# Spreading k's inverse norms through a DRAM row, and a new order of loads and PSUM buffers in the front

## Chip, cores and metric

One core of one Trainium2 chip runs the whole kernel. The metric is the device time of one execution in microseconds (us); the median of several runs counts.

## The reference

Two parts follow each other. A cross-covariance attention works on `q`, `k`, `v` of shape 4 x 6016 x 256 (batch, rows, channels), and a gated feed-forward layer works on its output, seen as 24064 x 256.

```python
def _attn_ref(q, k, v, tau):
    qn = q / (np.linalg.norm(q, axis=1, keepdims=True) + 1e-06)
    kn = k / (np.linalg.norm(k, axis=1, keepdims=True) + 1e-06)
    s = kn.transpose(0, 2, 1) @ qn / tau
    s = s - s.max(-1, keepdims=True)
    a = np.exp(s)
    a /= a.sum(-1, keepdims=True) + 1e-09
    return (v @ a).astype(np.float32)

def _moe_ref(x, w_gate, w_val, w_out):      # w_gate, w_val 256 x 1536, w_out 1536 x 256
    gate = 1.0 / (1.0 + np.exp(-(x @ w_gate)))
    val = x @ w_val
    return (gate * val @ w_out).astype(np.float32)
```

The norms run over the rows, so that there is one per channel and batch: 256 for q and 256 for k. The score matrix `s` is only 256 x 256 per batch. `tau` is 1.

## The kernel before

**Per batch.** The kernel computes the scores `q^T k` of a batch in PSUM (`ps_s`), squares q and k and sums the squares over the rows (`acc`, then a matmul with ones, `ps_n`). The root of the four columns of sums is `r` (128 partitions x 4: two columns for q, two for k), and `norms_inv` (L350) turns it into 1/(norm + 1e-6). q's inverse norm is a factor per partition of `ps_s`. k's inverse norm is a factor per column, so it has to be spread: every partition needs the whole row of 256 values. `scale_x` (L287) multiplies by both, `exps` (L388) takes the exponential, `row_sums` (L397) sums the rows, and twelve products `gh` (L452) multiply the exponentials with the two weight matrices. Thus G = a·w_gate and H = a·w_val are small matrices per batch, and v meets them directly.

**Per chunk.** v of a batch comes in 12 chunks (`ci`) of 4 x 128 rows, the last of 3 x 128. `load_v` (L144) loads a chunk on GpSimd's DMA queue, `transpose_v` (L458) transposes it, in all chunks but the first two by a transposing DMA on SP. For each of 12 blocks of 128 features (`f`), `glu` (L480) issues two gate matmuls into `ps_gate`, two value matmuls into `ps_val`, a tanh on ScalarE (`g_sb`, L501) and a multiply on VectorE (`hT`, L502). `ps_gate` and `ps_val` have two buffers each. The output product of the chunk before is spread over the same blocks, seven 128-column matmuls in each (`run_work`). It uses a scheme with fewer products, which needs sums of parts of `hT` on VectorE (`a_sum`, L524; in every block but f = 0 and f = 2) and additions on GpSimd.

**Order.** The instructions of each engine run in the order in which the program issues them. That order is written out by hand: `side_work` (L731) gives each piece of the next batch's attention a slot, and slot 12·ci + f is issued after block f of chunk ci. Scores, squares and sums of the next batch are done in chunks 0 to 7. From slot s0 = 98 on, so in chunk 8, follow the norms, in chunk 9 the spread and the exponentials, and up to the last block of chunk 11 the products `gh`, which must be there when the next batch begins. In this text (9,6) is block 6 of chunk 9. Batches 1, 2 and 3 are prepared in this way.

**The spread before.** `spread_both` (L300) multiplies r's column, broadcast over 128 columns, with a float32 identity, twice, on TensorE; `copy_rk` (L312) copies the result from PSUM into `rk_sb` on ScalarE. Batch 0 has functions of its own, `spread_k` and `weights`, and is prepared in the front, before any feed-forward work exists.

**The front.** All of q and k of batch 0 has to be loaded first (L151 to L177), then the first v chunk (L178), then the weights (L182 to L187), all on GpSimd's queue in this order. The first v chunk is transposed on TensorE into `ps_tp`, half of it is copied out by VectorE and half by ScalarE (L471 to L475, L723). `ps_tp` comes from the pool `psv` of two PSUM buffers, from which two of the first `gh` products (L727, L728) also take theirs. `row_sums` of the first half is issued between the transposes and VectorE's copy (the argument `then`, L474).

**PSUM.** Eight banks: two each for `psg`, `psv` and `pso`, and one each for `pss` (the scores, later half of the `gh` products) and `psm` (norms, the spread, row sums, the other half).

Of the kernel before, what the change touches and what calls it, by code (L numbers as in the profile page):

```python
# [9 lines left out]
FP32 = mybir.dt.float32  # L10
BF16 = mybir.dt.bfloat16
# [42 lines left out]
def kernel(  # L54
# [20 lines left out]
    nc = tc.nc  # L75
    P = nc.NUM_PARTITIONS
# [4 lines left out]
    B, N, C = q.shape  # L81
# [3 lines left out]
    CB = C // P  # L85
# [3 lines left out]
    TPC = 4  # L89
# [7 lines left out]
    def rows(x, b):  # L97
        return x[b].rearrange("(p t) c -> p t c", p=P)
# [3 lines left out]
    def pool(name, bufs, **kw):  # L102
        return ctx.enter_context(tc.tile_pool(name=name, bufs=bufs, **kw))
# [11 lines left out]
    spool = pool("spool", 1)  # L115
    mpool = pool("mpool", 2)
    opool = pool("opool", 2)
    psg = pool("psg", 2, space=PSUM)
    psv = pool("psv", 2, space=PSUM)
    pso = pool("pso", 2, space=PSUM)  # L120
    pss = pool("pss", 1, space=PSUM)
    psm = pool("psm", 1, space=PSUM)
# [3 lines left out]
    def mm(out, lhsT, rhs, start, stop, **kw):  # L126
        nc.tensor.matmul(out, lhsT=lhsT, rhs=rhs, start=start, stop=stop, **kw)  # L127
# [4 lines left out]
    def load_qk(b, t0, nt):  # L132

        tiles = []
        for name, src in (("q", q), ("k", k)):
            tl = qkpool.tile([P, 2 * TPC, C], BF16, tag=name, name=name + "_sb")
            nc.gpsimd.dma_start(out=tl[:, :nt, :], in_=rows(src, b)[:, t0 : t0 + nt, :])
            tiles.append(tl)
        for u in range(0, nt, TPC):
            qk[b, t0 + u] = [tl[:, u : u + TPC, :] for tl in tiles]  # L140
# [3 lines left out]
    def load_v(b, ci):  # L144
        t0, nt = groups[ci]
        v_sb = vpool.tile([P, TPC, C], BF16, tag="v", name="v_sb")
        nc.gpsimd.dma_start(out=v_sb[:, :nt, :], in_=rows(v, b)[:, t0 : t0 + nt, :])
        vs[b, ci] = v_sb
# [16 lines left out]
    ident_f = consts.tile([P, P], FP32)  # L165
# [9 lines left out]
    nc.scalar.copy(qk[0, 0][1], first_f32[1])  # L175
    for t0, nt in loads0[1:]:
        load_qk(0, t0, nt)  # L177
    load_v(0, 0)  # L178

    w_sb = [[consts.tile([P, CB, FG], BF16, name=f"w_{n}{fg}") for fg in range(NFG)] for n in ("gate", "val")]  # L180
    w_out_sb = consts.tile([P, FC, C], BF16)
    for fg in range(NFG):  # L182
        for w, src in enumerate((moe_w_gate, moe_w_val)):
            nc.gpsimd.dma_start(
                out=w_sb[w][fg],
                in_=src.rearrange("(t p) f -> p t f", p=P)[:, :, ds(fg * FG, FG)],
            )  # L187
    load_v(0, 1)

    w_sums = consts.tile([P, len(B_SUMS), FC // 2, P], BF16)  # L190
# [2 lines left out]
    for n in range(FC // TPC):  # L193
        w_f32[n] = f32pool.tile([P, TPC, C], FP32, tag="f32", name="w_f32")
        nc.gpsimd.dma_start(
            out=w_f32[n], in_=moe_w_out.rearrange("(t p) c -> p t c", p=P)[:, n * TPC : (n + 1) * TPC, :]
# [16 lines left out]
    st = {}  # L213

    def invert(out, x, eps, num):
        nc.vector.tensor_scalar(out=out, in0=x, scalar1=eps, scalar2=None, op0=ALU.add)
        nc.vector.reciprocal(out, out)
# [80 lines left out]
        )  # L298

    def spread_both(b):  # L300
        s = st[b]
        s["rk_ps"] = psm.tile([P, C], FP32, tag="m", name="ps_rk")
        for i in range(CB):
            mm(
                s["rk_ps"][:, ds(i * P, P)],
                s["r"][:, CB + i : CB + i + 1].to_broadcast([P, P]),
                ident_f,
                True,
                True,
            )  # L310

    def copy_rk(b):  # L312
        s = st[b]
        s["rk_sb"] = attp.tile([P, C], FP32, tag="rk", name="rk_sb")
        nc.scalar.copy(s["rk_sb"], s["rk_ps"])

    def norms_sqrt(b):
        s = st[b]
# [78 lines left out]
    def row_sums(b, i0, ni, pl, tag):  # L397
        s = st[b]
        ps_r = pl.tile([P, ni], FP32, tag=tag, name="ps_r")
        for i in range(ni):  # L400
            for j in range(CB):
                mm(
                    ps_r[:, i : i + 1],
                    s["e"][i0 + i][:, j, :],
                    ones_bf[:, 0:1],
                    start=(i == 0 and j == 0),
                    stop=(j == CB - 1),
                    skip_group_check=True,
                )
        r = attp.tile([P, ni], FP32, tag=f"rrow{i0}", name="rrow", bufs=2)  # L410
        invert(r, ps_r, 1e-9, 1.0)
        s.setdefault("rrow", []).extend(r[:, i : i + 1] for i in range(ni))
# [6 lines left out]
    def gh_tiles(b):  # L419
        st[b]["gh"] = [  # L420
            [ghpool.tile([P, CB, FG], BF16, tag=f"{n}{fg}", name=f"gh_{n}{fg}") for fg in range(NFG)]
            for n in ("G", "H")
        ]
# [28 lines left out]
    def gh(b, n, pl, tag, act=None):  # L452
        gh_store(b, n, gh_mms(b, n, pl, tag), n % 2 == 0 if act is None else act)
# [1 line left out]

    vts = {}

    def transpose_v(b, ci, ps=None, late=None, then=None):  # L458

        t0, nt = groups[ci]  # L460
        v_sb = vs.pop((b, ci))
        vT = vtpool.tile([P, TPC * CB, P], BF16, tag="vT", name="vT")
        flat = v_sb[:, :nt, :].rearrange("p t c -> p (t c)")
        if ps is None:
            nc.sync.dma_start_transpose(out=vT[:, : nt * CB, :], in_=flat)
        else:
            for n in range(nt * CB):
                nc.tensor.transpose(
                    out=ps[:, n, :], in_=flat[:, ds(n * P, P)], identity=ident_bf
                )  # L470
            half = nt * CB // 2 if late else nt * CB  # L471
            if late:
                late(vT[:, half : nt * CB, :], ps[:, half : nt * CB, :])
                then()  # L474
            nc.vector.tensor_copy(out=vT[:, :half, :], in_=ps[:, :half, :])  # L475
        vts[b, ci] = vT.rearrange("p (u cb) n -> p cb u n", cb=CB)

# [203 lines left out]
    for g, (t0, nt) in enumerate(groups0):  # L681
# [6 lines left out]
        while adds:  # L688
            w, last_sq = adds.pop()
# [26 lines left out]
    weights(0, 0)  # L716
    weights(0, 1)
    late = []
    ps_tp = psv.tile([P, TPC * CB, P], BF16, tag="v", name="ps_tp")
    gh_tiles(0)  # L720
    transpose_v(0, 0, ps_tp, lambda *a: late.append(a), lambda: row_sums(0, 0, 1, psm, "m"))
    gh(0, 0, psg, "g", act=True)
    nc.scalar.copy(*late.pop())  # L723
    half_row(0)
# [6 lines left out]
    def side_work(b):  # L731


        side = {}

        def at(slot, fn, *a):
            side.setdefault(divmod(slot, FC), []).append((fn, a))

        for ci in range(NCH):
            nb, nci = (b, ci + 1) if ci + 1 < NCH else (b + 1, 0)  # L740
            lb, lci = (b, ci + 2) if ci + 2 < NCH else (b + 1, ci + 2 - NCH)
            if (nb, nci) == (0, 1):
                at(8, lambda: transpose_v(0, 1, psm.tile([P, TPC * CB, P], BF16, tag="m", name="ps_tp")))
            elif nb < B:
                at(ci * FC + 2, transpose_v, nb, nci)
            if lb < B:
                at(ci * FC + 0, load_v, lb, lci)
            if (b, ci) == (0, 0):
                for i in range(FC // TPC):
                    at(8, copy_w_out, i)  # L750
                for n, m in enumerate((1, 0, 3, 2, 4)):
                    for i in range(FC // TPC):
                        at(10 + 2 * n, sum_w_out, m, i)
        n = b + 1
        if n == B:
            return side
        first, last = (14 if b == 0 else 0), 8 * FC
        for g, (t0, nt) in enumerate(groups):
            s0 = first + g * (last - first) // NCH
            if b == 0:  # L760
                at(max(0, s0 - 12), load_qk, n, t0, nt)
            elif s0 >= 24:
                at(s0 - 24, load_qk, n, t0, nt)
            for u in range(nt):
                at(first + (t0 + u) * (last - first) // NT, score, n, t0, u)
            if g == 0:
                at(s0, acc_start, n)
            for i, (fn, w) in enumerate(((acc_square, 0), (acc_add, 0), (acc_square, 1), (acc_add, 1))):
                at(s0 + 1 + 2 * i, fn, n, g, w)
        if n + 1 < B:  # L770
            for g, (t0, nt) in enumerate(groups[:3]):
                at(NCH * FC - 24 + 8 * g, load_qk, n + 1, t0, nt)
        s0 = 8 * FC + 2
        at(s0, norms_mm, n)
        at(s0 + 1, root_seed, n)
        at(s0 + 1, root_steps, n)
        at(s0 + 9, norms_inv, n)
        at(s0 + 10, spread_both, n)
        at(s0 + 11, copy_rk, n)
        at(s0 + 12, scale_x, n, 0)  # L780
        at(s0 + 13, scale_x, n, 1)
        at(s0 + 14, exps, n, 0)
        at(s0 + 15, exps, n, 1)
        at(s0 + 17, row_sums, n, 0, CB, psm, "m")
        at(s0 + 19, half_row, n)
        at(s0 + 17, gh_tiles, n)
        for i in range(len(gh_order)):
            at(s0 + 18 + 5 * i // 2, gh, n, i, *((pss, "s"), (psm, "m"))[i % 2])
        return side


# [66 lines left out]
```

## Time and profile before

| | |
|---|---|
| median of 3 runs | 808.96 us (808.84 to 809.2) |
| profiled execution | 808.89 us |
| its span in the trace | 807.1 us |
| granted TensorE clock | 0.998 |
| TensorE busy (PE) | 785.4 us, 97% |
| VectorE busy (DVE) | 709.1 us, 88% |
| ScalarE busy (ACT) | 525.7 us, 65% |
| GpSimd busy (POOL) | 355.2 us, 44% |
| HBM read and written | 78.64 and 24.64 MB |

The span is the time from the first to the last instruction of the program in the trace; 1.8 us of the execution lie around it. Busy time is the time in which an engine works on an instruction. PE is TensorE's matmuls, PEld its weight loads, SPq and POOLq the queues that issue DMAs. L127 is the helper `mm`, through which all matmuls go, so they are told apart by their tiles. "A <- B" after a wait says that A waited until B was done.

### The profile page before, as it was taken

What the parts mean: (1) busy time and instruction counts of PE and PEld (TensorE: products, weight loads), DVE (VectorE), ACT (ScalarE), POOL (GpSimd) and SP (SyncE); (2) the same over time, 40 slices, a digit from 0 to 9 for tenths busy, and PEclk for the clock granted to TensorE, in tenths of its full rate; (3) what the DMA queues carried; (4) which work ended last, traced back from release to release, by engine and by line L of the source; (5) the groups of instructions that cost most, each with busy time, mean ns of one, the idle gap of its engine ahead of it and who ended that gap; (6) DMA issues with size and microseconds to landing.
All of it is one profiled execution on the core that took longest, in us unless ns stands there. A gap on an engine that the chain in (4) does not pass through costs nothing.

```text
span 807.1 us, 17882 instructions
## 1 busy us (share of the span) xinstructions
PE 785.4 (97%) x6756; PEld 501.0 (62%) x6776; DVE 709.1 (88%) x1202; ACT 525.7 (65%) x891; POOL 355.2 (44%) x566
## 2 busy tenths in 40 slices
PE   4799999999999999999999999999999999999998
PEld 2556666666666666666666666666666566666666
DVE  5777999999879999998987999999988898898896
ACT  3667777766667776775666767776666665665664
POOL 4473545444552454335343544443534244444433
PEclk9999999999999999999999999999999999999999
DMA  9995758432666557422378486524222432432302
GB/s 214 206 207 98 130 91 139 94 67 46 105 129 122 88 109 139 86 53 67 73 118 132 75 142 113 104 54 91 62 53 54 87 65 61 85 66 66 83 30 74
DMA packets 77319, 78.24 MB, mean 97 GB/s; under 512 B 50736, under 2 KB 55088, under 8 KB 77232
## 3 DMA queue, kind: packets, MB, share of 16 engines
q0 software_dynamic: 21648, 39.59, 29.9%
q1 hardware_dynamic: 55008, 36.64, 19.8%
q8 instruction: 53, 0.87, 0.4%
q10 hardware_dynamic: 576, 0.85, 0.3%
q14 instruction: 34, 0.28, 0.1%
HBM read 78.64 MB, written 24.64 MB: 128 GB/s over the span
## 4 chain that ended last, share of the span: by engine, by line
PE 92%; DMA 4%; DVE 2%; issue 1%; ACT 1%; POOL 0%; POOLq 0%
PE ps_gate L127 29%; PE ps_val L127 29%; PE ps_o L127 27%; PE ps_s L127 4%; DMA k_sb<-in_k_dram 3%; PE ps_gh L127 2%; DMA w_gate<-in_moe_w_gate_dram 1%; DVE hT L502 1%; DVE sums L524 0%; ACT g_sb L501 0%; PE ps_rk L127 0%; DVE r L352 0%; DVE acc L278 0%; PE ps_end L127 0%; PE ps_n L127 0%
## 5 line engine op out<-in xcount | busy, mean ns | idle before, releaser
L501 ACT ACTIVATE g_sb<-ps_gate 128x512 f32<-128x512 f32 (+1 forms) x576 | 338.3, 588 | 228.5 <-PE ps_gate L127 220.7
L502 DVE SCALAR_TENSOR_TENSOR hT<-g_sb,ps_val 128x512 bf16<-128x512 f32 (+1 forms) x576 | 385.4, 672 | 78.9 <-ACT g_sb L501 69.5
L127 PE MATMUL ps_val<-vT,gh_H 128*128 128x512 bf16 (+1 forms) x1152 | 337.5, 375 | 0.3 <-DVE hT L502 0.3
L127 PE MATMUL ps_gate<-vT,gh_G 128*128 128x512 bf16 (+1 forms) x1152 | 337.5, 375 | 0.1
L524 DVE TENSOR_TENSOR sums<-hT 128x768 bf16<-128x768 bf16 (+1 forms) x460 | 278.6, 606 | 0.0
L127 PEld LDWEIGHTS <-sums 128*128 128x128 bf16 x2670 | 183.0, 98 | 82.1
L127 PEld LDWEIGHTS <-gh_H 128*128 128x128 bf16 x1152 | 112.7, 98 | 131.5 <-issue 0.8
L595 POOL TENSOR_TENSOR out_sb<-out_sb,m_sb 128x256 f32<-128x256 f32 x89 | 78.6, 883 | 234.3 <-ACT out_sb L585 205.7
L127 PE MATMUL ps_o<-w_sums,sums 128*128 128x128 bf16 x1602 | 154.4, 219 | 0.0
L127 PEld LDWEIGHTS <-hT 128*128 128x128 bf16 x1200 | 88.3, 98 | 46.8
L579 POOL TENSOR_TENSOR m_sb<-m_sb 128x128 f32<-128x128 f32 x89 | 42.0, 472 | 166.3 <-ACT m_sb L578 166.3
L127 PEld LDWEIGHTS <-gh_G 128*128 128x128 bf16 x1152 | 97.0, 98 | 14.9
L127 PE MATMUL ps_o<-w_out_sb,sums 128*128 128x128 bf16 x1068 | 96.2, 219 | 0.0
L127 PE MATMUL ps_o<-w_sums,hT 128*128 128x128 bf16 x1068 | 95.5, 219 | 0.0
L127 PE MATMUL ps_s<-k_sb,q_sb 128*128 128x256 bf16 x376 | 70.9, 293 | 13.7 <-DMA k_sb<-in_k_dram 7.2
L596 POOL TENSOR_TENSOR out_sb<-out_sb 128x256 f32<-128x256 f32 x89 | 76.4, 858 | 7.0
L585 ACT COPY out_sb<-ps_o 128x512 f32<-128x512 f32 x89 | 52.2, 586 | 12.7 <-PE ps_o L127 10.1
L278 DVE TENSOR_TENSOR acc<-acc,sq 128x1024 bf16<-128x1024 bf16 (+1 forms) x66 | 59.9, 907 | 0.0
L580 POOL TENSOR_TENSOR m_sb<-m_sb 128x128 f32<-128x128 f32 x89 | 54.4, 611 | 7.0
L240 ACT ACTIVATE sq<-k_sb 128x1024 bf16<-128x1024 bf16 (+2 forms) x44 | 44.8, 1027 | 12.2 <-DMA k_sb<-in_k_dram 12.0
L127 PEld LDWEIGHTS <-q_sb 128*128 128x128 bf16 x376 | 33.7, 105 | 19.7 <-issue 9.1
L578 ACT COPY m_sb<-ps_o 128x384 f32<-128x384 f32 x89 | 42.6, 479 | 3.4 <-PE ps_o L127 1.0
(78 smaller groups left out, 302.0 us busy)
## 6 DMA issues: line engine op xcount, KB each, us to landing
out_dram<-out_sb SPq DMA_DIRECT2D x43, 512.0 KB, 3.4
v_sb<-in_v_dram POOLq DMA_DIRECT2D x44, 256.0 KB, 5.2
q_sb<-in_q_dram POOLq DMA_DIRECT2D x35, 256.0 KB, 4.4
k_sb<-in_k_dram POOLq DMA_DIRECT2D x35, 256.0 KB, 6.1
q_sb<-in_q_dram POOLq DMA_DIRECT2D x4, 512.0 KB, 11.4
k_sb<-in_k_dram POOLq DMA_DIRECT2D x4, 512.0 KB, 13.3
w_f<-in_moe_w_out_dram POOLq DMA_DIRECT2D x3, 512.0 KB, 10.5
out_dram<-out_sb SPq DMA_DIRECT2D x3, 384.0 KB, 2.8
```

The costliest lines, as they stand in the source:

```text
L127: nc.tensor.matmul(out, lhsT=lhsT, rhs=rhs, start=start, stop=stop, **kw)
L240: nc.scalar.activation(out=sq[:, :nt, :], in_=src[:, :nt, :], func=ACT.Square)
L278: nc.vector.tensor_tensor(out=acc[:, :nt, :], in0=acc[:, :nt, :], in1=st[b]["sq", w][:, :nt, :], op=ALU.add)
L501: nc.scalar.activation(out=g_sb[:, :n], in_=ps_gate[:, :n], func=ACT.Tanh, scale=0.5)
L502: nc.vector.scalar_tensor_tensor(out=hts[b, ci][:, f, :n], in0=g_sb[:, :n], scalar=1.0, in1=ps_val[:, :n], op0=ALU.add, op1=ALU.mult,)
L524: nc.vector.tensor_tensor(out=sums[b, ci, g][:, m, :, : half * P], in0=hT[:, f0 + k0 : f1 : 2, ds(r0 * half * P, half * P)], in1=hT[:, f0 ...
L578: nc.scalar.copy(m, states[p]["ps"][:, : 3 * P].rearrange("p (n c) -> p n c", c=P))
L579: nc.gpsimd.tensor_tensor(out=m[:, 1, :], in0=m[:, 1, :], in1=m[:, 2, :], op=ALU.add)
L580: nc.gpsimd.tensor_tensor(out=m[:, 2, :], in0=m[:, 1, :], in1=m[:, 0, :], op=ALU.add)
L585: nc.scalar.copy(o[:, p : p + half + 1 : half, :], states[p]["ps"].rearrange("p (t c) -> p t c", c=C),)
L595: add(out=ends, in0=ends, in1=states[p]["m"][:, 1:3, :], op=ALU.add)
L596: add(out=ends, in0=ends, in1=mids, op=ALU.subtract)
```

## The change

In batches 1 to 3 `spread_both` writes the two columns of k's inverse norms with one DMA into a row of 256 float32 values in DRAM, and reads that row with a second DMA, broadcast to 128 partitions, into `rk_sb`. Both are issued on SP. `copy_rk` and the matmuls of the spread are gone. In the list of slots `norms_inv` and the spread come one slot later, `scale_x` four and three slots later (both in one slot), the exponentials, row sums, half_row and gh_tiles three slots later, and the twelve `gh` products begin three slots later and follow each other in steps of 9/4 of a slot instead of 5/2, so that the last is again in slot 143.

In the front the first v chunk is loaded after the first block of gate weights instead of before it; `ps_tp` comes from `pss`, whose bank held the scores of batch 0, instead of `psv`; and `row_sums` of the first half is issued after VectorE's copy of `vT` instead of before it.

```diff
--- before.py
+++ after.py
@@ -115,6 +115,7 @@
     spool = pool("spool", 1)
     mpool = pool("mpool", 2)
     opool = pool("opool", 2)
+    dpool = pool("dpool", 1, space=bass.MemoryType.DRAM)
     psg = pool("psg", 2, space=PSUM)
     psv = pool("psv", 2, space=PSUM)
     pso = pool("pso", 2, space=PSUM)
@@ -175,7 +176,6 @@
     nc.scalar.copy(qk[0, 0][1], first_f32[1])
     for t0, nt in loads0[1:]:
         load_qk(0, t0, nt)
-    load_v(0, 0)
 
     w_sb = [[consts.tile([P, CB, FG], BF16, name=f"w_{n}{fg}") for fg in range(NFG)] for n in ("gate", "val")]
     w_out_sb = consts.tile([P, FC, C], BF16)
@@ -185,6 +185,8 @@
                 out=w_sb[w][fg],
                 in_=src.rearrange("(t p) f -> p t f", p=P)[:, :, ds(fg * FG, FG)],
             )
+            if fg == 0 and w == 0:
+                load_v(0, 0)
     load_v(0, 1)
 
     w_sums = consts.tile([P, len(B_SUMS), FC // 2, P], BF16)
@@ -298,21 +300,12 @@
         )
 
     def spread_both(b):
-        s = st[b]
-        s["rk_ps"] = psm.tile([P, C], FP32, tag="m", name="ps_rk")
-        for i in range(CB):
-            mm(
-                s["rk_ps"][:, ds(i * P, P)],
-                s["r"][:, CB + i : CB + i + 1].to_broadcast([P, P]),
-                ident_f,
-                True,
-                True,
-            )
-
-    def copy_rk(b):
-        s = st[b]
+
+        s = st[b]
+        row = dpool.tile([C], FP32, tag="row", name="row")
+        nc.sync.dma_start(out=row.rearrange("(i p) -> p i", p=P), in_=s["r"][:, CB:])
         s["rk_sb"] = attp.tile([P, C], FP32, tag="rk", name="rk_sb")
-        nc.scalar.copy(s["rk_sb"], s["rk_ps"])
+        nc.sync.dma_start(out=s["rk_sb"], in_=row.rearrange("(o c) -> o c", o=1).to_broadcast([P, C]))
 
     def norms_sqrt(b):
         s = st[b]
@@ -455,7 +448,7 @@
 
     vts = {}
 
-    def transpose_v(b, ci, ps=None, late=None, then=None):
+    def transpose_v(b, ci, ps=None, late=None):
 
         t0, nt = groups[ci]
         v_sb = vs.pop((b, ci))
@@ -471,7 +464,6 @@
             half = nt * CB // 2 if late else nt * CB
             if late:
                 late(vT[:, half : nt * CB, :], ps[:, half : nt * CB, :])
-                then()
             nc.vector.tensor_copy(out=vT[:, :half, :], in_=ps[:, :half, :])
         vts[b, ci] = vT.rearrange("p (u cb) n -> p cb u n", cb=CB)
 
@@ -716,9 +708,10 @@
     weights(0, 0)
     weights(0, 1)
     late = []
-    ps_tp = psv.tile([P, TPC * CB, P], BF16, tag="v", name="ps_tp")
+    ps_tp = pss.tile([P, TPC * CB, P], BF16, tag="s", name="ps_tp")
     gh_tiles(0)
-    transpose_v(0, 0, ps_tp, lambda *a: late.append(a), lambda: row_sums(0, 0, 1, psm, "m"))
+    transpose_v(0, 0, ps_tp, lambda *a: late.append(a))
+    row_sums(0, 0, 1, psm, "m")
     gh(0, 0, psg, "g", act=True)
     nc.scalar.copy(*late.pop())
     half_row(0)
@@ -774,18 +767,17 @@
         at(s0, norms_mm, n)
         at(s0 + 1, root_seed, n)
         at(s0 + 1, root_steps, n)
-        at(s0 + 9, norms_inv, n)
-        at(s0 + 10, spread_both, n)
-        at(s0 + 11, copy_rk, n)
-        at(s0 + 12, scale_x, n, 0)
-        at(s0 + 13, scale_x, n, 1)
-        at(s0 + 14, exps, n, 0)
-        at(s0 + 15, exps, n, 1)
-        at(s0 + 17, row_sums, n, 0, CB, psm, "m")
-        at(s0 + 19, half_row, n)
-        at(s0 + 17, gh_tiles, n)
+        at(s0 + 10, norms_inv, n)
+        at(s0 + 11, spread_both, n)
+        at(s0 + 16, scale_x, n, 0)
+        at(s0 + 16, scale_x, n, 1)
+        at(s0 + 17, exps, n, 0)
+        at(s0 + 18, exps, n, 1)
+        at(s0 + 20, row_sums, n, 0, CB, psm, "m")
+        at(s0 + 22, half_row, n)
+        at(s0 + 20, gh_tiles, n)
         for i in range(len(gh_order)):
-            at(s0 + 18 + 5 * i // 2, gh, n, i, *((pss, "s"), (psm, "m"))[i % 2])
+            at(s0 + 21 + 9 * i // 4, gh, n, i, *((pss, "s"), (psm, "m"))[i % 2])
         return side
 
 
```

## The prediction

> **What bounds the kernel now.** I read the page's busy line first, then the waits, then the chain of waits around the places that the diff touches, then single stretches.
>
> ```profile
> PE 785.4 (97%) x6756; PEld 501.0 (62%) x6776; DVE 709.1 (88%) x1202; ACT 525.7 (65%) x891; POOL 355.2 (44%) x566
> PE 92%; DMA 4%; DVE 2%; issue 1%; ACT 1%; POOL 0%; POOLq 0%
> ```
>
> TensorE is busy for 97% and carries 92% of the chain that ended last. So time is won or lost only where TensorE is occupied or made to wait. Who makes it wait is in the waits of TensorE, and after the loads of the front one name is left:
>
> ```profile
> PEld ps_rk L127 <- DVE r L353: 2.9, 4, 0.8
> PE ps_rk L127 <- DVE r L353: 2.1, 4, 0.6
> ```
>
> Four times, one in the front and one each before batches 1, 2 and 3, TensorE waits for the reciprocal of the norms. The chain around the first later one (start, us, what):
>
> ```profile
> 183.87 0.45 PE ps_gate L127 x2
> 184.32 0.02 issue
> 184.34 0.61 ACT g_sb L501
> 184.95 0.02 issue
> 184.97 0.69 DVE hT L502
> 185.66 0.47 DVE sums L524
> 186.12 0.62 DVE r L352
> 186.75 0.02 issue
> 186.77 0.19 DVE r L353
> 186.96 0.04 issue
> 187.00 0.71 PE ps_rk L127 x4
> 187.71 0.43 PE ps_gate L127 x2
> ```
>
> The chain leaves TensorE at 184.3, goes through a tanh, hT, a sum and two small VectorE instructions and comes back at 187.00: the spreading matmuls stand in TensorE's queue before r exists. The timeline gives the price. Gate matmuls start every 1.25 us (182.45, 183.71, 184.96, and after it 187.55, 188.80, 190.06, 191.31). Only from 184.96 to 187.55 is it 2.59, so the spread costs 2.59 - 1.25 = **1.34 us**. The windows 379.29:381.88 and 573.63:576.22 hold the same 2.59 us and the same 19 matmuls, so it is paid three times, 4.02 us in all. Between them TensorE shows no other wait of that size.
>
> **What the Trainium skill says.** (1) "DMA: Bandwidth & Descriptors", section "Anatomy of one DMA", puts a fixed cost of about 2.0 us on a DMA (fitted on GpSimd's path), mostly the receipt of the write. The trace agrees roughly: the last 64 KB stores from SP and ACT landed in 1.8 and 1.5 us. (2) The same page, "Rules for kernel authors": a strided last dimension lowers to one descriptor per element, and a DMA that reads what another wrote must wait for its semaphore at the issuing engine. No run shows the first yet. (3) "SBUF — State Buffer", section "Who interferes with whom": VectorE and GpSimd exclude each other on a shared port, and VectorE's tensor_scalar is among the operations concerned. The trace agrees: L352 takes 692 ns in the later batches, 170 ns in the front where GpSimd only issues DMAs.
>
> **The change in the later batches.** Removed, three times: four float32 matmuls, their wait (1.34 us together, on the path) and ScalarE's copy rk_sb (366 ns; ScalarE is 65% busy, so worth nothing). Added: two DMAs on SP, the second waiting on SP for the first. The steps, with slot (9,f) for feature block f of chunk 9, and gates at 184.96 + 1.253 f now that nothing interrupts them:
>
> - r. norms_inv moves from (8,11) to (9,0). hT starts 1.26 us after its gate (183.71, 184.97), so at 186.22; it occupies VectorE for 0.60 (next start less own start). (9,0) has no sum. L352 starts at 186.82, takes 0.69 if GpSimd is in its way again, and L353 0.18: r at about 187.7. The next hT is due at 187.48, thus 0.2 late.
> - How late may hT be? It is done 0.69 us after its start, 1.95 after its gate; the second next ps_val needs its buffer 2 x 1.253 + 0.43 = 2.93 after that gate. About 0.95 us of lateness is free, so norms_inv costs nothing.
> - The trip. The row store is 256 elements of 4 bytes; nothing in the trace is like it. Nearest are the 64 KB stores, 1.5 and 1.8, and for the spread (128 rows of 1 KB) the 128 KB stores, 2.7. From below 1.5 + 1.8 = 3.3 us; from above twice the 4.1 us of the 512 KB store issued at 187.54, 8.2. I take 2.3 + 2.7 = 5.0: an estimate, 0.5 over the 64 KB store for its small elements. rk_sb lands at **192.7**, between 191.0 and 195.9.
> - Its user. Both scale_x move to (9,6): gate 192.48, hT 193.74, sum at 194.34 (0.47), scale_x at **194.8**. The slack of the trip is 2.1 us. The pair adds 2 x 0.40 to VectorE, so hT(9,7) starts at 195.60 and ends at 196.29; ps_val (9,9), at 192.48 + 3.76 + 0.43 = 196.67, needs it. 0.38 us are left: tight, but nothing. A sum that meets GpSimd took 0.85 for 0.55 at 191.92, which would leave 0.08.
> - ScalarE. The first exp waits for both scale_x, done near 195.7, so tanh (9,8), due at 195.6, ends near 196.7; gate (9,10) needs its buffer at 197.5. Hidden. The whole-block copy (0.59) and the second exp (0.51, each some 0.1 less in the queue) follow in that slot; tanh (9,9) then ends near 198.1, for gate (9,11) at 198.7.
> - SP's queue. Ahead of the two DMAs stands a store issued at 172.13, behind them the transposing load of chunk 10 and chunk 7's store:
>
> ```profile
> 172.13 0.33 SPq L637 DMA_DIRECT2D out_dram<-out_sb  x1
> 177.69 1.24 SPq L465 DMA_TRANSPOSE vT<-v_sb  x1
> 187.54 0.33 SPq L637 DMA_DIRECT2D out_dram<-out_sb  x1
> ```
>
>   The transpose waits for the row to land and goes out near 190.4 instead of 177.69; with 4.0 us to landing it is there at 194.4, and chunk 10 begins near 200. The store moves to about 192; its buffer is wanted in chunk 10's eighth block. GpSimd's queue is not passed; its v load at 187.46 shares the DMA engines.
> - Row sums, half_row and the gh products move three blocks later and go in 25 blocks instead of 28, with the last in the same block. Per 4.5 blocks VectorE needs 4.5 x (0.60 + 0.47 x 10/12) + 0.75 = 5.2 us, TensorE 4.5 x 1.253 + 2 x 0.43 = 6.5. Nothing.
>
> Sum: -3 x 1.34 = **-4.02 us**.
>
> **The change in the front.** Three edits: gate weights load before v, the transposed v goes to the bank of ps_s, and the first row sum follows both in TensorE's and VectorE's order.
>
> ```profile
> 34.15 0.61 PE L468 MATMUL ps_tp<-ident_bf,v_sb 128*128 128x128 bf16 x8
> 36.03 0.59 PE L127 MATMUL ps_gh<-w_gate,e_sb 128*128 128x512 bf16 x2 [0.18 <-DMA w_gate<-in_moe_w_gate_dram]
> 37.87 0.59 PE L127 MATMUL ps_gh<-w_val,e_sb 128*128 128x512 bf16 x2 [0.33 <-ACT vT L723]
> ```
>
> Now v lands at 33.5 (issue 26.75 + 6.7), its transposes fill time in which TensorE has nothing else, and w_gate lands at 36.0 (28.06 + 7.9), 0.18 us after it could be used. The new bank removes the 0.33 us wait: at most 0.5 gained. But the second of the two loads carries a delay. In the trace's packets 15 of w_gate's 16 engines report by 34.8, the last at 36.0, because a 16 KB instruction fetch held it from 33.8 for 0.89 us. Nothing before it in TensorE's order changes, so I expect the fetch at the same time, and v, now second, at 36.0. Then the transposes (0.61) start after the exps are ready (35.64) and stand ahead of the row sum and all gh products: first gh 36.7 for 36.03, VectorE's copy of vT (0.41) before the two inversions (0.35), gate (0,0) near 38.7 for 38.30. I take **+0.35**. Ends: -0.5 (v at 34.8) and +0.6 (the transposes' whole time).
>
> **Sum.** 808.89 (the profiled execution: span 807.1 and 1.8 around it) - 4.02 + 0.35 = 805.2; it lay 0.07 under the median 808.96, so 805.3.
>
> **Rivals.** A difference of 0.2%, 1.6 us, is about what a measurement here tells from no change.
> - *As above*, with stalls of at most 0.2 us per batch: 804.2 to 805.9. Chance 0.66.
> - *VectorE takes over part.* The pair of scale_x meets GpSimd's port, or the trip takes 8.2 us: 195.9 is 0.7 over the 195.2 that 194.8 and the slack allow. Each batch gives back 0.2 to 0.9: 805.9 to 808.0, mostly still faster. For it: the 0.08 us left above. Chance 0.15.
> - *The row is late: slower.* VectorE waits in order for rk_sb, behind it hT, behind that TensorE. If each small DMA queues with the v load of that moment (5.0 us to landing), the trip is 10, rk_sb at 197.7, 2.5 us over 195.2, less 1.34: +1.2 per batch, 808.96 + 3.5 + 0.35 = 812.8. It decides from a trip of 8.8 us. Against: the stores of that size. Chance 0.13.
> - *It doesn't do what it says*: the 0.9 us wait of r reappears on another engine and eats the gain, about 808.5. Against: in (9,0) VectorE has room. Chance 0.06.
>
> **Numbers.** Faster by over 0.2%: 0.66 + most of the second, 0.77. Slower: 0.13. Within: 0.10. The range runs from 804.1 (front at -0.5, no stall) to 808.0, the end of the second case; the slow case and some of the last stay out.
>
> **What would show it.** Right: no ps_rk in later batches; gates 1.25 us apart across 185 to 200; scale_x without a wait for rk_sb; row and rk_sb landing in about 5 us; v_sb landing near 36.0 and the first gate near 38.7. Wrong: VectorE's scale_x waiting for a DMA; the transposing load landing after chunk 10 has begun; TensorE waiting for hT in blocks 7 to 11; v landing at 34.8.

## The result, and the profile after

The changed kernel takes **830.51 us** (median of 5 runs, 829.19 to 831.69) against 808.96 before; the ratio is 1.0263, 95% interval 1.0249 to 1.0277. It is 21.5 us slower, where 805.3 was forecast. The profiled execution took 829.26 us with a span of 827.4, so 20.3 us more than the span before.

The page's busy line and the shares of the chain:

```profile
PE 788.6 (95%) x6764; PEld 500.6 (61%) x6764; DVE 709.0 (86%) x1202; ACT 525.0 (63%) x888; POOL 355.7 (43%) x566
PE 87%; DMA 9%; DVE 2%; issue 1%; ACT 1%; POOL 0%; DVEq 0%; ACTq 0%; POOLq 0%
```

The work is the same, but TensorE's share of the chain has fallen by five points and the DMAs' has risen by five. Who waits is in the waits, given as engine, line, what it waited for: total us, times, longest. First TensorE's, then VectorE's:

```profile
PE ps_val L128 <- DVE hT L494: 17.5, 4, 6.2
DVE x_sb L293 <- DMA rk_sb<-row: 18.4, 3, 6.7
```

Three times `scale_x` waits for the spread row, and TensorE, behind it, for the buffer that `hT` would free. (The fourth wait of TensorE, 0.3 us, was there before.) The chain of the first of the three, start, us, what:

```profile
187.29 0.59 DVE r L345
187.87 0.02 issue
187.90 0.19 DVE r L346
188.09 0.02 issue
188.10 8.28 DMA row<-r
196.38 0.02 issue
196.40 4.72 DMA rk_sb<-row
...
201.63 0.48 DVE x_sb L293
202.10 0.61 DVE hT L494
202.71 0.04 issue
202.75 1.01 PE ps_val L128 x2
203.76 0.75 PE ps_o L128 x7
204.51 0.85 PE ps_gate L128 x2
```

Two things are to be read here. The trip through DRAM takes 13.0 us (8.28 for the store of 1 KB, 4.72 for reading it back). And the matmuls after it are slow: a pair of gates takes 0.85 us where it took 0.43. The windows (stretch; length, busy time and number of instructions on PE, PEld, DVE, ACT and POOL; then the granted clock, DMA share, GB/s) say why:

```profile
196.00:200.00 4.00, 1.16 (x11) 0.65 (x10) 0.00 (x0) 0.00 (x0) 0.00 (x0) 1.00 0.06 22
202.75:205.55 2.80, 2.80 (x12) 1.44 (x12) 2.80 (x5) 1.90 (x5) 1.65 (x2) 0.50 0.28 63
206.00:207.00 1.00, 1.00 (x15) 0.64 (x13) 0.94 (x2) 0.09 (x1) 0.00 (x0) 1.00 0.00 0
403.50:406.90 3.40, 3.40 (x15) 1.72 (x15) 3.15 (x5) 2.35 (x5) 1.65 (x2) 0.50 0.27 60
603.72:608.30 4.58, 4.58 (x26) 2.63 (x26) 4.15 (x7) 2.34 (x5) 1.65 (x2) 0.50 0.26 49
```

After the idle stretch TensorE's clock is halved, and it is full again by 206; the last two lines show the same in the other two batches. The 20.3 us (20.25 before rounding) add up as follows: the front +0.3; three waits +17.2; three spreads on TensorE gone -4.0; the end +1.0 (the last gate comes 19.2 us later than before, the end 20.25); what is left, 5.7, is the time at half clock. The windows bear that last term out: in the three stretches TensorE is busy for 2.80 + 3.40 + 4.58 = 10.8 us at half clock, and half of that, 5.4 us, is lost.

### The profile page after: what moved, and what is told of

It reads as the page before. It is cut to its first block, busy times and chain, and to the rows that moved or that the text cites. A ratio compares the mean times of both kernels' runs of the same rounds, so it can differ in the third digit from the quotient of the medians.

```text
span 827.4 us, 17893 instructions
## 1 busy us (share of the span) xinstructions
PE 788.6 (95%) x6764; PEld 500.6 (61%) x6764; DVE 709.0 (86%) x1202; ACT 525.0 (63%) x888; POOL 355.7 (43%) x566
## 4 chain that ended last, share of the span: by engine, by line
PE 87%; DMA 9%; DVE 2%; issue 1%; ACT 1%; POOL 0%; DVEq 0%; ACTq 0%; POOLq 0%
PE ps_val L128 28%; PE ps_gate L128 28%; PE ps_o L128 25%; PE ps_s L128 4%; DMA row<-r 3%; DMA k_sb<-in_k_dram 3%; PE ps_gh L128 2%; DMA rk_sb<-row 2%; DMA v_sb<-in_v_dram 1%; DVE hT L494 1%; ACT g_sb L493 0%; DVE r L345 0%; DVE acc L280 0%; DVE x_sb L293 0%; DVE sums L516 0%
## 5 line engine op out<-in xcount | busy, mean ns | idle before, releaser
L128 PE MATMUL ps_s<-k_sb,q_sb 128*128 128x256 bf16 x376 | 68.9, 285 | 15.1 <-DMA k_sb<-in_k_dram 8.6
```

## The experiments

Each run was measured beside the kernel before, whose medians there are 809.04 to 809.08.

### The two halves apart

`e1_front_only` is the kernel before with the front's edits; `e2_spread_only` is the change with the front of before.

```diff
 e1: + if fg == 0 and w == 0: load_v(0, 0)        (and no load_v before the weights)
     + ps_tp = pss.tile(...);  row_sums(0, 0, 1, psm, "m") after transpose_v
 e2: + dpool, spread_both by two DMAs, later slots
```

> The kernel before with the front's edits alone (gate weights loaded before v, ps_tp in pss, row sum after the copy of vT); the spread stays on TensorE. Theory T (the loss is all in the later batches, the front costs 0.33 us because v is now the load that the instruction fetch holds up): first gate 0.3 us later, total 808.9 + 0.3 = 809.3. Rival R1 (the front's shift also sets off something later, such as loads that collide): 811 or more.

> The change with the front undone: k's norms through the DRAM row, later slots, front as before. Theory T: all of the loss but 0.3 us stays, 828.9 to 831.4, with scale_x waiting about 6 us for rk_sb in each of three batches. Rival R1: 826 or less.

Measured: e1 809.44 (ratio 1.0009, interval 1.0000 to 1.0018), its first gate 0.35 us later and everything after it by the same amount. e2 831.51 (1.0281, 1.0264 to 1.0298), with 20.2 us of VectorE's waiting for rk_sb. The whole loss is in the later batches; R1 falls.

### What the small store costs

`e3_probe` adds to the kernel before six small DMAs on SP, for which no computation waits.

```diff
+ at((ci + 1) * FC + 8, probe, b, kind)     # b = 1 to 3; one kind for each of chunks 1 to 6
```

> The kernel before, with six small DMAs on SP in block 8 of chunks 1 to 6 of batches 1 to 3, for which no computation waits and while no v load is due: A 256 x 4 bytes into one 1 KB DRAM row (the change's store), B 128 x 4 bytes into 512 bytes, C 128 x 8 bytes into 1 KB, D 256 x 4 bytes, each 512 bytes apart, E 128 x 8 bytes to SBUF, F the spread alone, 128 x 1 KB from the row. Their results are not used. Theory T1 (small writes into the same piece of DRAM are handled one after the other, so time to landing goes with their number): A 8, B and C about 5, D near 3 to 4, E about 2, F 4 to 4.7. Rival R2 (a DRAM write of less than 512 bytes has a long fixed receipt): A, B, C, D all about 8. Rival R3 (the v load in flight at that moment held the store up): A about 4, the others lower.

The DMA issues of this kernel (KB, median us to landing; halfrow is B, pairs C, apart D, sbcopy E, prk_sb F):

```profile
row<-r SPq DMA_DIRECT2D x3, 1.0 KB, 9.9
halfrow<-r SPq DMA_DIRECT2D x3, 0.5 KB, 10.6
pairs<-r SPq DMA_DIRECT2D x3, 1.0 KB, 7.7
apart<-r SPq DMA_DIRECT2D x3, 1.0 KB, 5.5
sbcopy<-r SPq DMA_DIRECT2D x3, 1.0 KB, 5.1
prk_sb<-row SPq DMA_DIRECT2D x3, 128.0 KB, 5.3
```

Each kind was issued three times in one execution, which took 809.07, as before. My places for them were not quiet: SP issued each of them 0.4 us after a store of 384 or 512 KB and 0.5 us after a v load. So 5.1 for a copy to SBUF is probably mostly queueing, and the absolute figures are too high. The comparison holds, since all of them stood behind such a store and a v load. D, with as many 4-byte writes as A, lands in little more than the copy to SBUF: neither the number of writes, nor their size, nor the neighbouring v load makes the store slow. R2 and R3 fall, and T1 as far as it counts writes: half as many (B) were not faster. What is left is how close together the elements lie.

`e9_probe_quiet` puts such stores on ScalarE's queue at other places.

```diff
+ at((ci + 1) * FC + 9, probe, b, kind)     # nc.scalar.dma_start
```

> The kernel before, with six small stores to DRAM on ScalarE's queue in block 9 of chunks 1 to 6 of batches 1 to 3, when no large transfer is due; nothing waits for them. The time from the end of the packets to the landing is what counts (5.4 to 8 us in the change, about 1 us with pairs). A 256 x 4 bytes in one row, as in the change: 16 adjacent partitions share 64 bytes. B pairs of 8 bytes: 8 partitions[...] fill 64 bytes. C 128 x 4 bytes, 8 bytes apart: as B, but 4 bytes each. D as B, shifted by 32 bytes[...]. E 128 x 4 bytes adjacent[...]. F 256 x 4 bytes, each 64 bytes apart. Theory T4 (what costs is that two DMA engines write parts of the same 64 bytes): A, D, E slow (4 us or more), B, C, F fast (about 1 us). Rival T3 (what costs is the number of writes to the same 64 bytes, whoever makes them): A and E slowest, B, C and D alike and half as slow, F fast. Rival R2 (every 4-byte write is slow): A, C, E, F slow, B and D fast.

In order A to F, KB and median us to landing:

```profile
row<-r ACTq DMA_DIRECT2D x3, 1.0 KB, 10.6
pairs<-r ACTq DMA_DIRECT2D x3, 1.0 KB, 4.9
every<-r ACTq DMA_DIRECT2D x3, 0.5 KB, 3.1
shifted<-r ACTq DMA_DIRECT2D x3, 1.0 KB, 3.2
halfrow<-r ACTq DMA_DIRECT2D x3, 0.5 KB, 9.9
every<-r ACTq DMA_DIRECT2D x3, 1.0 KB, 1.9
```

Again each kind was issued three times in one execution (809.19); A, C and E stood at the same distance behind the neighbouring loads of q and k, where there were any. The packets themselves are through 1.0 to 1.8 us after the issue (2.9 in one case of B and 2.0 in one of F). The rest is the time until the semaphore tells of the landing, called confirmation here: A 9.0 to 10.6, B 2.1 to 3.8, C 2.0 to 2.3, D 2.1 to 3.8, E 8.7 to 10.6, F 0.4 to 0.9. R2 falls with C and F. Rival T3 has the order right (A and E slowest, B, C, D alike, F fast), but in size it is wrong: with the elements twice as dense (8 to 4 bytes) the confirmation takes more than twice as long, some four times. T4 expected D slow and B fast, and they are alike. But D and B differ in T4's sense only if eight neighbouring partitions go through one DMA engine, and no trace here says which engine writes what. If four did, then four engines would write to the same 64 bytes in A and E, two in B, C and D, and one in F, which is also the order found. So it is shown that crowded elements are slow, not whether the number of writes or that of engines counts. How far apart they have to lie, and why the growth is so steep, stays open too.

### The same store in pairs, on the path

```diff
-        nc.sync.dma_start(out=row.rearrange("(i p) -> p i", p=P), in_=s["r"][:, CB:])
+        nc.sync.dma_start(out=row.rearrange("(p i) -> p i", p=P), in_=s["r"][:, CB:])
-            in1=s["rk_sb"],
+            in1=s["rk_sb"].rearrange("q (p i) -> q i p", p=P),   # in0 and out as "q (i p) -> q i p"
```

> The change with one difference: the row holds k's norms in pairs, so that each of 128 partitions writes 8 adjacent bytes (128 writes for 256), and scale_x reads rk_sb with a stride of two. Theory T3 (writes into the same small piece of DRAM are handled one after the other; in the separate measurement the pairs landed 1.9 to 2.5 us sooner): the row lands in about 6 us for 8.3, scale_x waits about 4 us for 6.1, 819 to 823. Rival R2 (fixed receipt of a small DRAM write): 829 to 831.

Measured: 809.40 (1.0004, 0.9996 to 1.0013), far better than either theory. From the DMA view of the two stores, minimum, median and maximum of row and spread together, and VectorE's wait:

```profile
DMA to landing us min/median/max: 3.4/3.8/4.6
DVE x_sb L293 <- DMA rk_sb<-row: 2.2, 3, 0.9
```

The row lands in 3.9, 4.6 and 3.8 us instead of 8.3, 9.6 and 8.4. In both kernels its packets end at the same point, 2.7 to 3.2 us after the issue; what changed is the confirmation after them, 5.3 to 6.8 before and 0.8 to 1.4 now. (I had taken the gain from e3's crowded queue, where it was 2.) The waits are now 2.2 us in all for rk_sb and 1.2 on TensorE, 0.3 of it there before, and no wait is long enough to cost the clock (mean 0.997). The same path with the same slots, and one access pattern, decides over 20 us: the slow landing of the row is the cause.

Why is e6 still no faster than before? The profiled execution, 808.10, is the fastest of twelve (up to 810.88). In it the gates gain 2.2 us in the three batches, where 4.0 was possible without any wait, and a front and an end that come 0.5 and 0.9 later take 1.4 back. What the other executions lose beyond that is not known.

### Time for the trip, and what stands behind it in SP's queue

`e4_users_later` leaves the slow store and moves all users six slots; `e5_time_for_trip` also moves chunk 10's transposing load ahead of it, and has the front of before.

```diff
 e4: + at(s0 + 22, scale_x, n, 0 and 1); exps, row_sums, half_row six slots later
     + at(s0 + 27 + 18 * i // 11, gh, ...)
 e5: + as e4;  at(s0 + 9, norms_inv, n);  at(s0 + 10, spread_both, n)
     + transpose_v of chunk 10 in slot 8 * FC + 8 instead of 9 * FC + 2
```

> The change, with all users of rk_sb six slots later (scale_x in block 0 of chunk 10, the gh products in 19 blocks instead of 25). rk_sb lands near 201.1, the users come near 202. Theory T (the loss is scale_x's wait): that wait is gone. But SP issues chunk 10's transposing load only after it has waited for the row, at 196.8, so it lands near 202, and chunk 10's first gate, due at 200.3, waits about 1.7 us: 808.9 + 0.3 - 4.0 + 3 x 1.7 = 810.3. Rival R4 (TensorE's stall has another source, the denser gh products or the order of VectorE): still over 820. If SP's queue does no harm: 805.2.

> The spread through the DRAM row with the front of before; norms_inv and the two DMAs one slot earlier than in the change, all users of rk_sb six slots later, and chunk 10's transposing load put into SP's order ahead of the two DMAs. Theory T (only the length of the trip and SP's order make the change slow): no wait for rk_sb, none for vT, no wait for the spread on TensorE, 809.0 - 3 x 1.34 = 805.0. Rival R4 (the denser gh products cost TensorE something too): 806 to 808, with TensorE waiting for hT or for a PSUM buffer in chunks 10 and 11. Rival R5 (the row is later still in some batch): over 808.

Measured: e4 817.91 (1.0105, 1.0090 to 1.0121), more than the 810.3 expected and under R4's 820. Of TensorE's waits, and of SP's timeline:

```profile
PE ps_gate L128 <- DMA vT<-v_sb: 8.1, 3, 3.8
188.21 0.38 SPq L306 DMA_DIRECT2D row<-r  x1
197.22 0.33 SPq L308 DMA_DIRECT2D rk_sb<-row  x1
197.65 1.24 SPq L458 DMA_TRANSPOSE vT<-v_sb  x1
```

`scale_x` no longer waits. SP sits at the second DMA until the row has landed, and the transposing load behind it, which before went out at 177.69, comes 20 us later and too late for chunk 10: TensorE waits 2.3, 3.8 and 2.0 us, for 1.7 expected, and after the longest of these it is busy for 5.9 us at half clock. e5 takes this away too: 806.09 (0.9963, 0.9950 to 0.9977), with neither rk_sb nor vT among TensorE's waits. Its gates are 1.09, 1.33 and 1.34 us earlier per batch; the 805.0 expected is missed because the end comes later (below). R5 falls. R4's 806 to 808 holds the number but not its reason: TensorE waits neither for hT nor for a PSUM buffer in chunks 10 and 11. Why the first batch gains 0.25 less than the others is not known. The slow trip itself costs TensorE nothing where time is left for it.

### The bubble before, and the front

`e7_tensor_spread_later` keeps the spread on TensorE and issues it one slot later. `e8_front_v_first` keeps two of the front's edits and loads v first.

```diff
 e7: - at(s0 + 10, spread_both, n)
     + at(s0 + 11, spread_both, n)               (copy_rk, scale_x, exps one slot later)
 e8: + ps_tp = pss.tile(...);  row_sums after transpose_v
```

> The kernel before with the spreading matmuls one slot later behind norms_inv (and copy_rk, scale_x and exps one slot later). Theory T6 (the bubble of 1.34 us is 0.79 us of waiting for r, and 0.55 us of matmuls): the wait goes, the matmuls stay, 809.0 - 3 x 0.79 = 806.6. Rival: the wait moves to another place in VectorE's row of work, 809.

> The kernel before with two of the front's three edits (ps_tp in pss, row sum after the copy of vT), but v loaded first as before. Theory T7 (the front loses by v's late landing alone; the other edits remove the 0.33 us wait for ScalarE's copy of vT): the transposes run near 34.5, first gate near 37.9 for 38.3, 808.5. Rival: no gain, 809.0, because ScalarE's and VectorE's evictions of gh set the first gate.

Measured: e7 806.61 (0.9970, 0.9959 to 0.9982). Its chain at the old place of the bubble:

```profile
187.22 0.39 PE ps_o L127 x7
187.62 0.50 PE ps_rk L127 x4
188.12 0.43 PE ps_gate L127 x2
```

The wait is gone and the matmuls cost 0.50. So 0.84 of the 1.34 us was waiting, and one slot of distance buys it without any DMA. e8 808.64 (0.9995, 0.9986 to 1.0003): the sign is as expected, but it is not clear of the measurement's spread. In its profiled execution the loads of the front themselves came about 0.4 us later, and the first gate still 0.15 earlier than before.

### Together

```diff
+ pairs;  at(s0 + 9, norms_inv, n);  at(s0 + 10, spread_both, n);  transpose_v of chunk 10 ahead
+ at(s0 + 18, scale_x, n, 0 and 1);  exps to half_row two slots later;  at(s0 + 23 + 2 * i, gh, ...)
+ the front of e8
```

> What the runs so far point to, together: pairs in the row, norms_inv and the two DMAs one slot earlier than in the change, chunk 10's transposing load ahead of them on SP, users of rk_sb two slots later, and the front with v loaded first but the other two edits. Theory (each part as measured): 809.05 - 3 x 1.34 - 0.4 = 804.6, plus up to 0.8 us at the end, where the spread without TensorE's matmuls shifts an instruction fetch onto the last store (seen in all kernels without them): 804.6 to 805.4, faster than e7's 806.6. Rival R4 (denser gh products stall TensorE): 806 or more.

Measured: 805.53 (0.9957, 0.9943 to 0.9971), the lowest median of all, 0.1 above the range expected. It is clear of the kernel before but not of e5 and e7, whose intervals overlap its own; so the times do not show that the pairs and the new front add anything to e5. Its gates come 1.34 us earlier in each of the three batches, -4.46 us in all with the front. The span gains 3.5 only, because the end gives 1.0 back.

## Why the prediction was wrong

The sign that the prediction named first for being wrong, scale_x waiting for a DMA, is what the profile shows.

**The step that failed** is the trip, and in it the row store: "I take 2.3 + 2.7 = 5.0". It measured 8.28 + 4.72 = 13.0 in the first batch, 9.63 + 4.02 and 8.38 + 4.42 in the others. Of the 8.0 us of error in the first, 6.0 are the store's and 2.0 the spread's. rk_sb came at 201.1 for 192.7. The path behind it was right: with a trip of 13.0 the prediction's own sum puts rk_sb at 200.7, 5.5 us past the 195.2 that it allowed, and TensorE waited 5.6 (6.2 and 5.4 in the other batches).

**The upper bound failed too.** 8.2 us was twice the landing of a 512 KB store. I had written that nothing in the trace is like 256 elements of 4 bytes, and then bounded it by something unlike it: the large stores took longer with their bytes (1.5 us for 64 KB, 4.1 for 512 KB), this one by the confirmation of writes that lie close together, which no row of the trace held. A bound "from above" has to be above in the quantity that decides.

**The rival "the row is late" came out, by another cause.** Its chain was right word for word: scale_x waits in order, behind it hT, behind that TensorE. Its price, +1.2 per batch, came from queueing with the v load, and the queue is not the cause (e3's D is fast behind the same loads, and e9's A slow where no v load runs). Rather it goes the other way: that v load landed 7.2 us after its issue for 5.0 before, although its packets ended no later than the row's. e6, with pairs in the row, has this load at the same place, 0.3 us ahead of the store, and its packets end at about the same time (3.1 to 3.5 us after the issue, 3.0 to 3.2 in the change). Here are its KB and its us to landing in the first batch, in the change and then in e6:

```profile
v_sb<-in_v_dram POOLq DMA_DIRECT2D x1, 192.0 KB, 7.2
v_sb<-in_v_dram POOLq DMA_DIRECT2D x1, 192.0 KB, 4.0
```

In the other two batches it took 8.7 and 6.8 us in the change, 4.7 and 4.0 in e6. So the slow store holds up the landing of a load that was issued before it. The Trainium skill, "DMA: Bandwidth & Descriptors", section "Queues, rings and completion order", has a reason: the increment of a semaphore waits for every earlier write of that DMA engine, across its queues. The figures agree with it.

**What the sum left out: the clock.** A wait of this length has a second price. The Trainium skill, "TensorE: Matmul & The Clock Gate", section "What's actually happening", says that after an idle window of about 3.4 us the clock falls to half, until a window of work has passed. The trace agrees: 0.50 after the waits of the change, 5.4 to 6.2 us, and in e4 0.50 after the wait of 3.8 us, but 1.00 after those of 2.3 and 2.0. That is 1.4 to 2.3 us per batch, not in my sum at any end.

**What it also left out: the end.** In the six kernels here without the spread's matmuls the last instruction comes 0.9 to 1.3 us later after the last gate than in the kernel before. The sum had nothing for it, so that even a trip of 5.0 us would have given about 806.3 for 805.3, an estimate from these figures. A slip without consequence: the lower end of the range, 804.1, does not follow from its terms, since 808.96 - 4.02 - 0.50 is 804.4.

**What held.**

- The bubble: 1.34 us, three times. Gates in e10 come earlier by just that in each batch, in e5 by 1.09, 1.33 and 1.34, and e7 divides it into 0.84 of waiting and 0.50 of matmuls.
- r at 187.7: 188.1, of which 0.3 is the front's.
- The front: +0.35 forecast, +0.33 measured, by the mechanism named. v, loaded second, landed at 35.9, its last DMA engine 1.1 us after the others, and the instruction fetch of 16 KB ran again from 33.8. Two lines of the timeline:

```profile
35.97 0.62 PE L461 MATMUL ps_tp<-ident_bf,v_sb 128*128 128x128 bf16 x8 [1.68 <-DMA v_sb<-in_v_dram]
38.63 0.59 PE L128 MATMUL ps_gate<-vT,gh_G 128*128 128x512 bf16 x2 [0.21 <-ACT vT L716]
```

- The slack of `scale_x`, 0.38 us after 194.8: in e6 rk_sb lands at 196.1. With e6's shift of 0.5 that is 0.8 late, of which the slack leaves 0.4; the next gate comes 0.53 late.
- The denser gh products cost nothing: neither e5 nor e10 shows TensorE waiting there.

**What was right in form and wrong in time.** SP's order: I let the transposing load go out at 190.4 and land in time. It went out at 196.8 and would have been the next wait, as e4 shows; here it was hidden behind the longer wait of scale_x.

## What to carry to other kernels

A transfer that no row of the profile resembles has to be measured before its price goes on a critical path; the packets' own time, 1 to 3 us here, says nothing about when its semaphore arrives. Small values that have to go through DRAM are better written as pairs per partition, and their order undone where they are read (e6). When a DMA chain replaces work on the bounding engine, count where its waiting instruction stands in the issuing queue and what is behind it: e4 lost 8 us of waiting to that alone. And where an engine waits for a value that is nearly ready, issuing its instruction a slot later (e7) got two thirds of the gain with no new resource.

## What the runs showed that I had not expected

- Small DRAM writes whose elements lie 4 bytes apart are confirmed 9 to 11 us after their packets in e9 and 5 to 7 in the change; in e9 those 8 bytes apart take 2 to 4, those 64 bytes apart under 1. 128 of them cost as much as 256.
- Counted from the issue the figure is steadier. On SP the store of 4-byte elements lands in 8.3 to 10.7 us, with its packets through at 3 us in the change and at 1.1 to 1.3 in e5. The pairs land in 3.8 to 4.6, with packets through at 3 us in e6 and at 1.0 to 1.3 in e10. So the 0.8 to 1.4 of e6 is not what pairs cost in general.
- What was issued behind such a store was late as well. The v load 0.5 us behind it landed in 11.0 to 11.6 us in e5, and in 6.0 to 6.7 in e10 with pairs, for 4.4 to 5.0 before. No wait of TensorE came of it.
- A broadcast read of that 1 KB row to 128 partitions landed in 3.2 to 5.0 us in the kernels that use it (5.0 to 5.8 in e3's crowded queue), for 2.7 of a 128 KB store.
- At the end of the kernels without the spread's matmuls the last stores are slower: in e10 the last 64 KB store landed in 2.15 us for 1.55. In these six kernels an instruction fetch of 16 KB runs during the last 64 KB stores, in the six with the matmuls none does. That explains at most 0.6 of the 1.0 us, and that the fetch is the reason is not shown.
